# Attention over a compressed memory, then a SwiGLU layer: the column of ones that sums the exponentials is made 32 columns wide

## The chip, the core and the metric

The kernel runs on one core of one Trainium2 chip. Its engines work side by side, each through its own queue in order: TensorE (PE; its weight loads are listed apart, as PEld), VectorE (DVE), ScalarE (ACT), GpSimd (POOL), and SyncE (SP), which issues the DMAs. On-chip data lie in SBUF; TensorE writes its results to PSUM. The metric is the time of one execution on the device, in microseconds, as the median of several runs. A profile is one further execution, recorded by the hardware profiler.

## The reference

Eight batches of eight heads with 576 tokens of 64 values. For each of 32 memory slots, a softmax of `phi` over the tokens weighs k and v into a summary row, 32 rows a head; q attends to those rows; the result, 4608 tokens of 512 values, goes through an RMS norm and a SwiGLU layer of width 1536. All is float32.

```python
def _attn_ref(q, k, v, phi):
    a = phi - np.max(phi, axis=2, keepdims=True)
    a = np.exp(a)
    a = a / (np.sum(a, axis=2, keepdims=True) + 1e-09)
    k_m = np.einsum('bhsm,bhsd->bhmd', a, k)
    v_m = np.einsum('bhsm,bhsd->bhmd', a, v)
    ...
    return np.matmul(attn, v_m)

def _moe_ref(x, w_gate, w_val, w_out, rms_g):
    ...
    g = xn @ w_gate
    silu = g * (1.0 / (1.0 + np.exp(-g)))
    val = xn @ w_val
    return (silu * val @ w_out)
```

(What is left out first is the scores of q against `k_m` and their softmax over the slots, `attn`; then the RMS norm.) `phi` is laid out with axis 2 as the 576 tokens, so the sum in the third line of `_attn_ref` runs over the tokens: one number for each head and slot.

## The kernel before

**Stages.** The batches are numbered 0 to 7 and worked on in pairs. For each batch the kernel loads `phi`, k and v (`load_phi`, `load_kv`), takes the maximum of `phi`, subtracts it and exponentiates (`prep`), and multiplies the exponentials with k and v (`kv_steps`). Queries are scored against the result (`q_steps`, `score_steps`), normed (`x_steps`), and multiplied with the weights of the SwiGLU layer (`vw_steps`, `gv_steps`, `out_steps`). The weights come in as `raw` and are split by integer arithmetic on DVE into two halves of lower precision (`convert`, with lines 413 to 443 on DVE). In the first 165 us these stages overlap; from there on nearly all is the SwiGLU layer, with some attention of the last two pairs in between.

**Order.** The order of the instructions is written out by hand. Each step has a number, its place; all steps are sorted by place and issued in that order. `K_AT` has the places of the eight batches' products, `KP` the distance of two of their six chunks, and `POST` the places of what follows them: `sums`, `post1`, `turn`, `post2`, `self_products`, `post3`. SP issues the loads in an order of its own, each behind the one before.

**The sums.** `e_bd` holds a batch's exponentials, for four pairs of heads and nine groups of 128 rows (64 tokens of each of the two heads), as 128 x 64 blocks whose columns are the 32 slots of each head. `chunk` (line 787) multiplies each block with the 128 columns of k and v of the same rows and adds them up in the PSUM tile `kvp`, columns 0 to 127; even and odd pairs (`par`) go to the upper and the lower 64 rows of the tile, which are two column halves of TensorE's array. `prep` (line 764) has POOL add some of the nine blocks together into `es`; `ESN` says how many such additions there are for a batch. `sums` (line 802) then multiplies what is left, 7, 5 or 3 blocks for each pair of heads, with a tile `ones` of 128 x 1, and adds them up in column 128 of `kvp`. All products of one pair of heads follow each other before the next pair's, in the other half, begin. Over all batches that is 36 blocks for each of four pairs, 144 products.

**What reads them.** `post1` (lines 810 to 814) adds 1e-9 to column 128 and writes that to column 129 (`si`), takes the reciprocal (`ri`), and scales columns 0 to 127 with it (`kn`). `turn` (line 824) transposes `kn`, and `post2` copies it to `km` and `vt`, for the scores and for the SwiGLU layer.

Of the kernel before, what the change touches and what calls it, by code (L numbers as in the profile page):

```python
# [8 lines left out]
F32 = mybir.dt.float32  # L9
# [10 lines left out]
WB = 4  # L20
PRM = dict(
    LK=150,
    V0=169.536,
    V0S=[-7.546, 0.266, 0.444],
    G0=[3.08, 8.562, 9.611, 9.895],
# [83 lines left out]
def kernel(  # L109
# [26 lines left out]
    P = 128  # L136
# [13 lines left out]
    persist = ctx.enter_context(tc.tile_pool(name="persist", bufs=1))  # L150
# [380 lines left out]
    def vw_steps(i, vp_tile=None):  # L531

        ps_, u, pr, j = where(i)

        def mm(cc):
            def f():
                if cc == 0:
                    vp_[i] = vp_tile() if vp_tile else ps.tile([P, 2, 2, 256], F32, tag="vw", name=f"vp{i}", bufs=1)
                vp = vp_[i]
                vh, vl = vm[pr][:, 0], vm[pr][:, 1]  # L540
                wh, wl = (x.rearrange("p hp g f -> p hp (g f)") for x in wsplit[ps_ * NJ + j])
                for e in range(2):
                    def lhs(vt):
                        return vt[:, cc, e].rearrange("p o x -> p (o x)")
                    for n, (l, r) in enumerate(((vh, wh), (vh, wl), (vl, wh))):
                        nc.tensor.matmul(  # L546
                            vp[:, cc, e, :], lhs(l), r[:, 2 * cc + e, :],
                            start=(n == 0), stop=(n == 2),
                        )
            return f  # L550

        def evac():
            vp = vp_.pop(i)
            xh, xl = (x.rearrange("p e c f -> p c e f") for x in slot(i))
            for h in range(2):
                rows = slice(64 * h, 64 * h + 64)
                src = vp[rows, :, ::-1, :] if h else vp[rows]
                nc.scalar.copy(xh[rows], src)  # L558
                urgent.append(nc.vector.tensor_tensor(  # L559
                    out=xl[rows], in0=src, in1=xh[rows].bitcast(F32), op=ALU.subtract  # L560
                ).ins)
        return [mm(0), mm(1), evac]
# [61 lines left out]
    with ExitStack() as c1:  # L624
# [5 lines left out]
        c1k = ExitStack()  # L630
        sk = c1k.enter_context(tc.tile_pool(name="sbk", bufs=2, side="right", reuse_waits="tile"))

        ones = persist.tile([P, 1], F32, name="ones")
        nc.vector.memset(ones, 1.0)
        a_tiles = {0: sa.tile([P, NT, 256], F32, name="a0", bufs=1)}

# [38 lines left out]
        def load_kv(b, hp):  # L675
            if b in HOME:
                if ("kvx", b, hp // 2) not in st:
                    st["kvx", b, hp // 2] = persist.tile(
                        [P, 2, 2, S], F32, tag=f"at{'hl'[hp // 2]}{HOME[b]}", name=f"kv{b}_{hp // 2}x"
                    )  # L680
                t = st["kvx", b, hp // 2][:, hp % 2]
            else:
                t = sk.tile([P, 2, S], F32, tag="kv", name=f"kv{b}_{hp}", bufs=PRM["KB"])
            for i, src in enumerate((k, v)):
                load(
                    t[:, i, :],
                    src[b, 2 * hp:2 * hp + 2].rearrange("h (p c) d -> (h p) (c d)", c=NT),
                )
            st["kv", b, hp] = t
# [86 lines left out]
        def kv_steps(b):  # L776
# [18 lines left out]
            def sums():  # L795
                kvp = st["kvp", b]
                for cc in range(2):
                    for par in range(2):
                        hp = 2 * cc + (par ^ j)
                        es = st["es", b]  # L800
                        for i, x in enumerate(es):
                            nc.tensor.matmul(
                                kvp[64 * par:64 * par + 64, cc, 128:129],
                                x[:, hp, :], ones, start=(i == 0), stop=(i == len(es) - 1),
                            )

            def post1():
                kvp = st["kvp", b]
                si = kvp[:, :, 129:130]
                nc.vector.tensor_scalar_add(si, kvp[:, :, 128:129], 1e-9)  # L810
                ri = sb.tile([P, 2, 1], F32, tag="ri", name=f"ri{b}")
                nc.vector.reciprocal(ri, si)
                st["kn", b] = kn = sb.tile([P, 2, P], F32, tag="kn", name=f"kn{b}")
                nc.vector.tensor_tensor(
                    out=kn, in0=kvp[:, :, 0:P], in1=ri.broadcast_to([P, 2, P]), op=ALU.mult
                )
# [58 lines left out]
            for cc in range(2):  # L875
                for c0 in range(0, NT, 3):
                    steps.append(chunk(cc, c0, c0 + 3))
            return steps, [sums, post1, turn, post2, self_products, post3], store

        def q_steps(pr, s):  # L880
# [94 lines left out]
        def place(base, offsets, steps):  # L975
            assert len(offsets) == len(steps)
            return [(base + o, f) for o, f in zip(offsets, steps)]
# [8 lines left out]
        for b in range(B):  # L986
            steps, post, store = kv_steps(b)
            if b >= 2 * G:
                ev.append((max(K_AT[b] + 6 * PRM["KP"] + PRM["POST"][5] + PRM["VD"][b - 2 * G], PRM["LK"]), store))
            ev += place(K_AT[b], [PRM["KP"] * i for i in range(6)], steps)  # L990
            ev += place(K_AT[b] + 6 * PRM["KP"], PRM["POST"], post)
            for hp in range(HP):
                if (b, hp) > (0, 1):
                    ev.append((min(K_AT[b] + PRM["KD"][b * HP + hp], PRM["LK"] - 0.1), lambda b=b, hp=hp: load_kv(b, hp)))
            if b == 0:
# [26 lines left out]
        def s_tile(name, shape):  # L1022
            return ps_s.tile(shape, F32, tag="S", name=name, bufs=PRM["B"][2])
        ev += place(PRM["V0"], PRM["V0S"], vw_steps(0, lambda: s_tile("vp0", [P, 2, 2, 256])))
        gv0 = gv_steps(0, lambda name: s_tile(name, [P, 1024]))
        ev += place(PRM["V0"], PRM["G0"], [gv0[x] for x in (0, 1, 3, 4)])
        if PRM["E1"]:
            ev += place(PRM["V0"], PRM["V1"], vw_steps(1, lambda: s_tile("vp1", [P, 2, 2, 256])))
        close = K_AT[B - 1] + 6 * PRM["KP"] + 0.1
# [298 lines left out]
```

## Time and profile before

| what | value |
|---|---|
| timed runs (3) | 857.08, 855.59, 855.20 us; median 855.59 us |
| the profiled execution | 850.64 us |
| its span, first to last instruction | 848.9 us |
| granted TensorE clock, mean over the span | 0.989 |
| busy: PE, weight loads, DVE, ACT, POOL | 812.3, 731.9, 537.0, 403.7, 322.9 us |
| DMA | 131.62 MB, mean 155 GB/s |

The page of the profile has, after the busy times, one line for each engine with its busy share in 40 equal slices, and the clock that TensorE was granted in them. Its fourth part follows the chain that ended last back from the last instruction: at each step to what released it, or to the instruction before it on its engine. A group of instructions is told by line, engine, operation and tiles (`out<-in`, the program's names without their numbers), with partitions x columns of the array for TensorE, the size of what it streams, and the count; behind the bar stand busy time, the mean duration of one in ns, and the idle time of the engine just before. Matmuls are pipelined and overlap, so durations of neighbours don't add up, and where one half of the array works beside the other two of them run at once. A few per cent of the matmul records can be missing.

### The profile page before, as it was taken

How to read it: one execution, taken by the hardware profiler on the slowest of the kernel's cores; microseconds unless marked ns; L12 is line 12 of the kernel's file. 1: busy time of each engine (PE TensorE's matmuls, PEld its weight loads, DVE VectorE, ACT ScalarE, POOL GpSimd, SP SyncE). 2: the span in 40 equal slices, each digit the busy share in tenths (PEclk: the TensorE clock that was granted, in tenths of full speed). 3: DMA queues.
4: the chain of work that ended last, by engine and by line, in shares of the span. 5: the costliest groups of instructions: out<-in, count | busy, mean ns of one | idle time of the engine just before them, and what ended most of it. 6: DMA issues, size and time to landing. Idle time of an engine off the chain costs nothing.

```text
span 848.9 us, 16232 instructions
## 1 busy us (share of the span) xinstructions
PE 812.3 (96%) x6234; PEld 731.9 (86%) x6234; DVE 537.0 (63%) x940; ACT 403.7 (48%) x731; POOL 322.9 (38%) x279
## 2 busy tenths in 40 slices
PE   5989997999999999999999989999999999999997
PEld 4878886889989889988989888899999999999996
DVE  5697868876678898979889546312354454444434
ACT  2767647687565465656454423354333223232220
POOL 3565746734444563643544512411212122121220
PEclk9889999999999999999999999999999999999999
DMA  9997525545343543743534567806736357264437
GB/s 335 364 383 271 201 72 152 149 117 153 115 119 96 167 124 78 189 132 104 150 111 130 176 144 198 239 15 168 180 94 179 77 149 199 59 153 88 100 100 174
DMA packets 99493, 131.62 MB, mean 155 GB/s; under 512 B 42324, under 2 KB 61784, under 8 KB 99416
## 3 DMA queue, kind: packets, MB, share of 16 engines
q1 hardware_dynamic: 99416, 130.59, 54.6%
q8 instruction: 49, 0.80, 0.4%
q14 instruction: 28, 0.23, 0.1%
HBM read 73.93 MB, written 31.46 MB: 124 GB/s over the span
## 4 chain that ended last, share of the span: by engine, by line
PE 74%; DVE 9%; DMA 5%; ACT 3%; issue 3%; POOL 3%; SPq 2%; ACTq 0%; POOLq 0%; DVEq 0%
PE po L1120 31%; PE pg L586 14%; PE pv L586 14%; PE vp L546 3%; PE vq L1059 3%; PE kvp L787 2%; SPq L1102 1%; DVE xl L559 1%; DMA kv_0x<-in_k_dram 1%; DVE mi L438 1%; DVE ex L413 1%; DVE ex L416 1%; PE S L1199 1%; PE xp L280 1%; ACT xh L558 1%
## 5 line engine op out<-in xcount | busy, mean ns | idle before, releaser
L614 POOL TENSOR_TENSOR hl<-hf,hh 128x512 fp32r<-128x512 f32 (+1 forms) x86 | 124.5, 1449 | 285.7 <-ACT hh L613 285.6
L1128 DVE TENSOR_TENSOR acc<-po,acc 128x512 f32<-128x512 f32 x180 | 123.5, 688 | 124.2 <-PE po L1120 123.5
L1120 PE MATMUL po<-oh,hh 128*128 128x512 f32 x387 | 154.1, 399 | 4.5 <-DVE at L246 1.9
L1120 PE MATMUL po<-ol,hh 128*128 128x512 f32 x387 | 153.3, 396 | 0.5 <-DMA ol<-od 0.5
L1120 PE MATMUL po<-oh,hl 128*128 128x512 f32 x387 | 151.5, 391 | 0.0
L595 DVE TENSOR_TENSOR hf<-pv,sg 128x320 f32<-128x320 f32 (+1 forms) x188 | 83.4, 452 | 88.4 <-PE pv L586 64.3
L594 ACT ACTIVATE sg<-pg 128x320 f32<-128x320 f32 (+1 forms) x188 | 76.6, 410 | 123.4 <-PE pg L586 115.2
L586 PE MATMUL pg<-ath,xh 128*128 128x320 f32 (+1 forms) x376 | 85.9, 301 | 3.9 <-ACT sg L594 3.6
L1120 PEld LDWEIGHTS po<-oh,hh 128*128 128x128 f32 x387 | 73.0, 189 | 16.9 <-DVE at L246 2.1
L1120 PEld LDWEIGHTS po<-oh,hl 128*128 128x128 f32 x387 | 73.0, 189 | 16.1
L586 PE MATMUL pg<-ath,xl 128*128 128x256 f32 (+1 forms) x376 | 83.8, 297 | 0.7 <-DMA xl<-sl 0.7
L613 ACT CAST hh<-hf 128x512 fp32r<-128x512 f32 (+1 forms) x86 | 57.4, 672 | 55.2 <-DVE hf L595 37.6
L586 PE MATMUL pv<-ath,xl 128*128 128x256 f32 (+1 forms) x376 | 82.9, 296 | 0.0
L586 PE MATMUL pg<-atl,xh 128*128 128x256 f32 (+1 forms) x376 | 82.9, 297 | 0.0
L586 PE MATMUL pv<-ath,xh 128*128 128x320 f32 (+1 forms) x376 | 82.2, 298 | 0.4 <-DVE hf L595 0.3
L586 PE MATMUL pv<-atl,xh 128*128 128x256 f32 (+1 forms) x376 | 81.6, 296 | 0.0
L1120 PEld LDWEIGHTS po<-ol,hh 128*128 128x128 f32 x387 | 73.1, 189 | 9.0 <-DMA ol<-od 0.7
L462 POOL TENSOR_TENSOR w<-mi,ex 128x512 f32<-128x512 f32 x34 | 43.9, 1290 | 84.8 <-ACT mi L450 54.6
L586 PEld LDWEIGHTS pg<-ath,xh 128*128 128x128 f32 x376 | 62.6, 189 | 9.2 <-ACT sg L594 4.3
L559 DVE TENSOR_TENSOR xl<-vp,xh 64x1024 fp32r<-64x1024 f32 x48 | 58.5, 1219 | 16.4 <-ACT xh L558 15.6
L586 PEld LDWEIGHTS pv<-ath,xh 128*128 128x128 f32 x376 | 61.6, 189 | 3.6 <-DVE hf L595 0.9
L586 PEld LDWEIGHTS pg<-ath,xl 128*128 128x128 f32 x376 | 62.2, 190 | 2.8 <-DMA xl<-sl 0.9
(163 smaller groups left out, 1519.7 us busy)
## 6 DMA issues: line engine op xcount, KB each, us to landing
xh<-sh SPq DMA_DIRECT2D x96, 128.0 KB, 3.7
xl<-sl SPq DMA_DIRECT2D x80, 128.0 KB, 3.1
out_dram<-acc SPq DMA_DIRECT2D x72, 128.0 KB, 2.4
raw<-in_moe_w_gate_dram SPq DMA_DIRECT2D x12, 512.0 KB, 4.0
raw<-in_moe_w_val_dram SPq DMA_DIRECT2D x12, 512.0 KB, 3.8
raw<-in_moe_w_out_dram SPq DMA_DIRECT2D x12, 512.0 KB, 4.0
wd<-whl SPq DMA_DIRECT2D x24, 256.0 KB, 3.8
whl<-wd SPq DMA_DIRECT2D x12, 512.0 KB, 5.3
```

What stands on the lines that cost most here:

```text
L462: (nc.gpsimd if on_pool else V).tensor_tensor(out=d["w"], in0=m, in1=ex, op=ALU.mult)
L546: nc.tensor.matmul(vp[:, cc, e, :], lhs(l), r[:, 2 * cc + e, :], start=(n == 0), stop=(n == 2),)
L559: urgent.append(nc.vector.tensor_tensor(out=xl[rows], in0=src, in1=xh[rows].bitcast(F32), op=ALU.subtract).ins)
L586: nc.tensor.matmul(pt[:, :N], l[cc][:, b, half * P:half * P + P], r[:, cc, b, t0:t0 + n, :].rearrange("p t x -> p (t x)"), start=(m == 0), ...
L594: nc.scalar.activation(sg[:, :N], pg[:, :N], AF.Silu)
L595: urgent.append(nc.vector.tensor_tensor(out=hf[:, :, b, :], in0=pv[:, :N].rearrange("p (t x) -> p t x", x=64), in1=sg[:, :N].rearrange("p ...
L613: nc.scalar.copy(hh, hv)
L614: nc.gpsimd.tensor_tensor(out=hl, in0=hv, in1=hh.bitcast(F32), op=ALU.subtract)
L787: nc.tensor.matmul(kvp[64 * par:64 * par + 64, cc, 0:128], e_bd[j][:, hp, c, :], st["kv", b, hp][:, :, 64 * c:64 * c + 64], start=(c == 0) ...
L1059: nc.tensor.matmul(vp[:, h, e, :], vall[a][:, cc, k:k + 4, :].rearrange("p q m -> p (q m)"), w, start=(a == 0), stop=(a == 1),)
L1120: nc.tensor.matmul(po, l[:, tt, :], r, start=(m == 0), stop=(m == 5))
L1128: nc.vector.tensor_tensor(out=accs[key], in0=po, in1=accs[key], op=ALU.add).ins
```

## The change

The tile `ones` becomes 128 x 32, all 1.0, and so each product in `sums` writes 32 equal columns, 128 to 159, in place of column 128 alone. `post1` still reads column 128; its own column `si` moves from 129 to 160. The tile `kvp` has 256 columns for each two pairs of heads, so it doesn't grow.

```diff
 PRM = dict(
     LK=150,
+    W1=32,
...
-        ones = persist.tile([P, 1], F32, name="ones")
+        ones = persist.tile([P, PRM["W1"]], F32, name="ones")
         nc.vector.memset(ones, 1.0)
...
                             nc.tensor.matmul(
-                                kvp[64 * par:64 * par + 64, cc, 128:129],
+                                kvp[64 * par:64 * par + 64, cc, 128:128 + PRM["W1"]],
                                 x[:, hp, :], ones, start=(i == 0), stop=(i == len(es) - 1),
                             )
 
             def post1():
                 kvp = st["kvp", b]
-                si = kvp[:, :, 129:130]
+                si = kvp[:, :, 128 + PRM["W1"]:129 + PRM["W1"]]
                 nc.vector.tensor_scalar_add(si, kvp[:, :, 128:129], 1e-9)
```

## The prediction

> **What bounds the kernel now.** I read the page first: the span and the chain of waits by engine.
>
> ```profile
> span 848.9 us, 16232 instructions
> ...
> PE 74%; DVE 9%; DMA 5%; ACT 3%; issue 3%; POOL 3%; SPq 2%; ACTq 0%; POOLq 0%; DVEq 0%
> ```
>
> The chain is TensorE for three quarters of the span, so anything that slows TensorE or its clock there counts. Next come the instructions that read the ones (the view by tile; min/median/max in ns, then first and last start), and the sums' pieces of the chain in order of time (start, length).
>
> ```profile
> L802 PE MATMUL kvp<-ones,e_bd x160: 197/197/246, 18.1 to 124.1; 128*64 128x1 f32 x160
> L802 PE MATMUL kvp<-ones,es x128: 167/197/218, 17.8 to 124.0; 128*64 128x1 f32 x128
> ```
>
> ```profile
> 69.56 1.80 PE kvp L802 x38
> ...
> 72.39 0.73 PE kvp L802 x11
> ...
> 73.29 0.59 PE S L918 x18
> ...
> 94.90 0.68 PE kvp L802 x19
> ...
> 105.14 0.68 PE kvp L802 x19
> ```
>
> There are 160 + 128 = 288 matmuls of one column, two instructions for each fp32 product, each with its own weight load of 64 columns, and all in the first 125 us. On the later chain lie 38 + 11 + 19 + 19 = 87 of them, in 3.89 us, between other pieces of TensorE. (S is there for a comparison below.)
>
> Then I read the clock by stretches, cut where it changes; the columns are start:end, length, busy time of PE, weight loads, DVE, ACT and POOL, clock, DMA share and GB/s.
>
> ```profile
> 16.97:20.39 3.42, 3.42 (x72) 3.23 (x69) 2.62 (x3) 1.17 (x2) 0.00 (x0) 1.00 1.08 395
> 20.39:27.21 6.82, 5.73 (x53) 5.38 (x54) 3.83 (x11) 4.63 (x4) 3.81 (x3) 0.50 0.96 329
> 27.21:47.69 20.48, 17.95 (x320) 15.72 (x317) 15.74 (x25) 17.03 (x33) 11.08 (x12) 1.00 1.06 379
> 47.69:54.52 6.83, 6.28 (x59) 5.10 (x59) 6.71 (x12) 4.09 (x12) 5.07 (x6) 0.50 1.07 383
> 146.68:150.09 3.41, 3.41 (x12) 2.83 (x12) 3.09 (x6) 3.41 (x8) 2.99 (x2) 0.50 0.00 0
> ```
>
> Half clock is granted three times, for 6.82, 6.83 and 3.41 us, so the clock seems to be judged in windows of 3.41 us. Ahead of the first drop stands a window in which PE counts as busy for all of its 3.42 us.
>
> **What the change adds: wider matmuls.** Each of the 288 streams 31 columns more. What a column costs is bounded by two neighbouring rows, with the same 64-column weights and 64 or 128 columns streamed.
>
> ```profile
> L918 PE MATMUL S<-km,qT x288: 219/223/368, 32.8 to 97.6; 128*64 128x64 f32 x144
> L787 PE MATMUL kvp<-kv,e_bd x216: 272/273/323, 34.5 to 123.3; 128*64 128x128 f32 x108
> ```
>
> By the first a column is (223 - 197) / 63 = 0.41 ns, by the second (273 - 197) / 127 = 0.60 ns: 13 to 19 ns of duration for 31 columns. What the path pays is the spacing, not the duration. The weight loads of the first group of sums show that:
>
> ```profile
> 18.03 0.49 PEld L802 LDWEIGHTS kvp<-ones,e_bd 128*64 128x64 f32 x7
> ```
>
> Seven loads in 0.49 us overlap heavily. With some 0.14 us for the last, they start (0.49 - 0.14) / 6 = 58 ns apart, all in one column half of the array. S switches halves at every product and does 18 in 0.59 us, 33 ns each, so at most 66 ns apart in one half, with 64 columns. From 1 to 64 columns the spacing in a half thus grows by at most 8 ns, and 31 columns are half of that: at most 4 ns, 87 x 4 = 0.35 us. A streaming time of 13 ns fits into the 58 ns that go by between two loads anyway. I take 1 ns: **+0.1 us**. The upper end is that nothing hides: 87 x 13 = 1.1 us to 87 x 19 = 1.7 us. The lower end is that wide sums issue as densely as S does, 3.89 us - 87 x 33 ns = 1.0 us less. I don't take it, since S gets its 33 ns from switching halves at every step, which the sums still won't do.
>
> The rest is small. The memset writes 32 columns instead of one, once, while the first loads are on their way: nothing, and some tens of ns if that cover were gone. The last matmul of a group ends 13 to 19 ns later ahead of DVE, in the three or four groups on the chain: **+0.05 us**. The `si` column moves within its tile, and DVE's operations on it keep their shapes. No wait, DMA or buffer is added, and no queue changes its order.
>
> **What the change moves: the clock.** The columns streamed in a window tell more than the busy time does. These are the matmuls from 16.97 to 20.39 us, after which the clock fell; then those of the window from 68.17 to 71.58 us, after which it held (groups by form: count, busy us, mean ns, idle before).
>
> ```profile
> L802 PE MATMUL kvp<-ones,e_bd 128*64 128x1 f32 x39 | 2.5, 198 | 0.0
> L802 PE MATMUL kvp<-ones,es 128*64 128x1 f32 x16 | 1.6, 202 | 0.0
> L787 PE MATMUL kvp<-kv_1x,e_bd 128*64 128x128 f32 x12 | 1.1, 277 | 0.0
> L733 PE MATMUL mr<-ident,mx 128*64 128x128 f32 x4 | 0.4, 272 | 0.0
> ```
>
> ```profile
> L802 PE MATMUL kvp<-ones,e_bd 128*64 128x1 f32 x30 | 1.9, 197 | 0.0
> L802 PE MATMUL kvp<-ones,es 128*64 128x1 f32 x12 | 1.1, 198 | 0.0
> L787 PE MATMUL kvp<-kv_1x,e_bd 128*64 128x128 f32 x10 | 0.9, 283 | 0.0
> L897 PE MATMUL qtp<-ident,qr 128*128 128x128 f32 x5 | 0.8, 284 | 0.0
> L218 PE MATMUL tp<-ident,a 128*128 128x128 f32 x3 | 0.5, 291 | 0.0
> ```
>
> The first streams 55 + 16 x 128 = 2,103 columns, the second 42 + 18 x 128 = 2,346. With 32 columns the first has 55 x 32 + 2,048 = 3,808. So I expect **no drop at 20.39 us**. Against this reading stands the third drop. Its window, from 143.27 us on, has at least 8 x 256 columns of these two kinds, and up to 512 of a third that starts at its end, so up to 2,560, and still lost the clock, with 1.9 us of plain idling in it: columns alone aren't the whole rule.
>
> ```profile
> L586 PE MATMUL pg<-ath,xh 128*128 128x256 f32 x4 | 0.9, 311 | 0.0
> L546 PE MATMUL vp<-whl,vm 128*128 128x256 f32 x4 | 0.6, 282 | 0.0
> L1120 PE MATMUL po<-oh,hh 128*128 128x512 f32 x1 | 0.6, 598 | 1.9 <-DVE at L246 1.9
> ```
>
> In the Trainium skill's "TensorE: Matmul & The Clock Gate", the section "What's actually happening" has the gate follow how busy the PE has been. If that meant matmuls in flight, the full window at 16.97 could not have lost the clock, and the change would leave the clock alone; by the rows, one-column matmuls count for little. Either way the sum below comes out the same to 0.1 us.
>
> For the price of that drop is nearly nothing. The products of the second batch run in it:
>
> ```profile
> L787 PE MATMUL kvp<-kv_0x,e_bd 128*64 128x128 f32 x36 | 4.1, 421 | 0.0
> ```
>
> At full clock that would be about half, so what follows on PE could come some 2 us sooner. But who is late next? DVE, whose pieces are here, with SP's issue of a load and, from the view of the DMA issues, its size and its us to landing:
>
> ```profile
> 34.58 1.36 DVE L742 TENSOR_TENSOR phi<-phi,mr 128x1152 f32<-128x1152 f32 x1 [1.34 <-PE mr L733]
> 35.85 0.47 DVE L413 TENSOR_SCALAR ex<-raw 128x512 int32<-128x512 int32 x1
> ```
>
> ```profile
> 28.93 0.38 SPq L348 DMA_DIRECT2D raw<-in_moe_w_gate_dram  x1
> ```
>
> ```profile
> raw<-in_moe_w_gate_dram SPq DMA_DIRECT2D x1, 512.0 KB, 6.8
> ```
>
> ```profile
> DVE ex L430 <- ACT ex L419: 0.2, 1, 0.2
> ```
>
> DVE's wait for PE, 1.34 us up to 34.58, would go. But the raw weights land at 28.93 + 6.8 = 35.7 us, and L413 reads them at 35.85. The queues already move 379 GB/s at a share of 1.06 there, so the load can't land sooner. From L413 on DVE waits for others only once up to 63 us, 0.2 us for ACT (the last fence, of the waits from 34.6 to 63 us). So the gain is **-0.1 us** at L413; if DVE found other inputs, up to 2 us. The drop at 47.69 comes while DVE is the late one and stays.
>
> **The sum** against the profiled execution's 850.64 us (848.9 of span, 1.7 around it): + 0.1 + 0.05 - 0.1, no change. The median of the timed runs, 855.59 us, lies 4.95 us above that execution; carried over, the forecast is **855.5 us**.
>
> **The rivals.** *Faster: a drop that this profile just missed.* A window laid from 69.6 to 73.0 us, 1.4 us later than the one above, holds this:
>
> ```profile
> L802 PE MATMUL kvp<-ones,e_bd 128*64 128x1 f32 x38 | 2.5, 197 | 0.0
> L802 PE MATMUL kvp<-ones,es 128*64 128x1 f32 x12 | 1.2, 202 | 0.0
> L218 PE MATMUL tp<-ident,a 128*128 128x128 f32 x4 | 0.7, 286 | 0.0
> L897 PE MATMUL qtp<-ident,qr 128*128 128x128 f32 x4 | 0.6, 272 | 0.0
> ```
>
> That is 50 + 8 x 128 = 1,074 columns, half of what lost the clock at 20.39; with 32 columns 2,624. If the windows lie otherwise in other executions, the old kernel loses half of 3.41 us (1.7 us), or of two windows (3.4 us), in a stretch where the chain is TensorE, and the new one doesn't. For it: the timed runs spread over 1.9 us and lie above the profiled one. Against it: one profile can't show that the windows move, and DVE and ACT may take up part. In the same section the Trainium skill calls the window free-running; nothing in this trace can show that. Time: 855.6 - 1.7 = 853.9 to 855.6 - 3.4 = 852.2 us. Chance 0.30.
>
> *Slower: the columns aren't hidden.* If the next weight load in a half waits until the last column has streamed, the 87 sums on the chain pay 13 to 19 ns each: 856.7 to 857.3 us. It passes 0.2% (1.7 us, about what a measurement of this kernel can tell from no change) at 20 ns each. For it: the sums run several times in a row in one half. Against it: S, at 66 ns with 64 columns. Chance 0.10, with whatever else turns out worse in the order of waits.
>
> *It does nothing to the clock.* The drop at 20.39 stays, because PE idles soon after the sums anyway (5.73 us busy of 6.82). The time is 855.6 and falls into the forecast: a third of its chance.
>
> **How the numbers follow.** Same 0.60 (853.9 to 857.3), faster 0.30, slower 0.10. The range reaches down over the faster rival, two windows lost before and none after, to 852.0, and up to the middle of the slower one, 857.0.
>
> **What would show it.** The sums' loads still 58 ns apart in a half, and 38 of them in about 1.8 us, show the columns hidden; 71 ns or more shows the slower rival. Full clock from 20.39 to 27.21 us with L413 still near 35.8 us shows the cap. I would be wrong if DVE's work after 36 us moved forward with PE, or if the clock of the two kernels differs near 72 us from one execution to the next.

## The result

The changed kernel takes 862.22 us (median of 9 runs, 857.37 to 865.33), the kernel before 855.59 us in the same comparison: a ratio of 1.007 with an interval of 1.0048 to 1.0093. It is slower, by about 6.6 us, and outside the forecast range. Its profiled execution took 859.45 us. The page of the profile of the changed kernel, span and chain by engine:

```profile
span 857.7 us, 16234 instructions
...
PE 78%; DVE 8%; ACT 4%; POOL 3%; DMA 3%; issue 2%; SPq 2%; POOLq 0%; DVEq 0%; ACTq 0%
```

The work is the same but for the wider products; lines behind 23 have moved down by one. The view by tile shows the products themselves (min/median/max in ns):

```profile
L803 PEld LDWEIGHTS kvp<-ones,e_bd x160: 132/138/227, 19.3 to 130.2; 128*64 128x64 f32 x160
L803 PE MATMUL kvp<-ones,e_bd x160: 192/223/294, 19.4 to 130.2; 128*64 128x32 f32 x160
L635 DVE MEMSET ones<- x1: 85/85/85, 0.8 to 0.8; 128x32 f32 x1
```

A product lasts 223 ns where it lasted 197, but that is duration, not spacing. The chain of waits of the changed kernel, in order of time (start, length), has this piece:

```profile
111.32 0.68 PE kvp L803 x19
```

Nineteen sums in 0.68 us, as before (105.14 and 94.90 there). The columns are hidden; that isn't where 6 us went.

**Where they went.** The last sums of batch 3 end at 60.96 us before and at 59.77 after: the changed kernel is ahead. Those of batch 5 end at 95.57 and 101.74, and from there to batch 7 both need 28.7 us. So about 7.4 us are lost between 60 and 102 us (41.97 us from batch 3 to batch 5 in place of 34.61). Behind batch 7 the changed kernel needs 727.3 us, the kernel before 724.6 in this profile and 727.3 in a second one (experiment e8), so that part needn't be the change's. The waits of TensorE from 60 to 102 us in the changed kernel (us in total, times, longest):

```profile
PE qtp L898 <- ACT qT L906: 1.8, 1, 1.8
PE mr L734 <- DVE mx L725: 1.6, 1, 1.6
PE xp L281 <- ACT at L229: 1.1, 1, 1.1
PE mt L717 <- DVE mc L710: 0.6, 1, 0.6
PE qtp L898 <- DVE at L229: 0.3, 1, 0.3
```

and those from 60 to 98 us in that second profile of the kernel before:

```profile
PE qtp L897 <- DVE at L228: 0.7, 1, 0.7
PE xp L280 <- ACT at L228: 0.7, 1, 0.7
PE kvt L824 <- DVE kn L814: 0.4, 1, 0.4
```

5.4 us of waiting in place of 1.8, for other producers. The two programs hold the same operations on every engine. What changed is the order in which they stand. The launch at the end of the file (line 1324) builds the program so:

```python
    with _tile.TileContext(nc, schedule_with_timeline_sim=True) as tc:
```

The places that the kernel section above calls the order are only the order in which the program hands its instructions over. A scheduler then orders them, by modelled times as its name says; that a product of 32 columns has another modelled time than one of a single column is what e3 and e4 below bear out. The two built programs differ in their order on every engine. On PE the differences run from the 97th to the 642nd of 5,288 matmuls (an fp32 product, which the trace shows as two instructions, counts once), on DVE from the 19th to the 128th of 940 operations: from the first batch's sums to batch 5's products. On PE ahead of batch 4's products (lines of the changed kernel; before at the left, after at the right):

```
L717 mt  (maxima, batch 5)               L717 mt
L825 kvt x8                              L734 mr x2
L788 kvp, products of batch 4 x15        L898 qtp_0_4 x4
L734 mr x2                               L825 kvt x8
L898 qtp_0_4 x4                          L788 kvp, products of batch 4 x9
```

Ahead of the first score `S` of the next pair there stand more transposes and `xp` products than before (8 `xp`, 5 `qtp` and 4 `tp` more). And at batch 5 the transpose `qtp_3_8` stands ahead of all products; before, it stood behind the first 17.

### The profile page after: what moved, and what is told of

It is laid out like the page before. It is cut to its first block, busy times and chain, and to the rows that moved or that the text cites. A ratio compares the mean times of both kernels' runs of the same rounds, so it can differ in the third digit from the quotient of the medians.

```text
span 857.7 us, 16234 instructions
## 1 busy us (share of the span) xinstructions
PE 819.1 (96%) x6234; PEld 734.0 (86%) x6234; DVE 537.2 (63%) x940; ACT 403.9 (47%) x731; POOL 322.2 (38%) x279
## 4 chain that ended last, share of the span: by engine, by line
PE 78%; DVE 8%; ACT 4%; POOL 3%; DMA 3%; issue 2%; SPq 2%; POOLq 0%; DVEq 0%; ACTq 0%
PE po L1121 32%; PE pg L587 15%; PE pv L587 15%; PE vp L547 4%; PE vq L1060 3%; PE kvp L788 3%; SPq L1103 1%; PE S L1200 1%; DVE mc L710 1%; PE kvp L803 1%; DVE xl L560 1%; DMA phi<-in_phi_dram 1%; PE gv L587 1%; PE tp L219 1%; PE xp L281 1%
## 5 line engine op out<-in xcount | busy, mean ns | idle before, releaser
L614 ACT CAST hh<-hf 128x512 fp32r<-128x512 f32 (+1 forms) x86 | 57.4, 672 | 55.0 <-DVE hf L596 37.5
```

The lines of the kernel that those rows point to most:

```text
L614: nc.scalar.copy(hh, hv)
```

## The experiments

Where the width of the sums had to be set apart from the order, the sums were widened or narrowed after the order was settled:

```python
def _set_width(nc, n):
    ...
    i = copy.replace(i, ins=[wide(i.ins[0]), *i.ins[1:]], outs=[wide(i.outs[0])])
```

so that all instructions stand as they would with the other width. "Old order" is that of the kernel before, "new order" that of the changed one.

### e1: 32 columns in the old order

```diff
-                                kvp[64 * par:64 * par + 64, cc, 128:128 + PRM["W1"]],
-                                x[:, hp, :], ones, start=(i == 0), stop=(i == len(es) - 1),
+                                kvp[64 * par:64 * par + 64, cc, 128:129],
+                                x[:, hp, :], ones[:, 0:1], start=(i == 0), stop=(i == len(es) - 1),
...
+    _set_width(nc, 32)
```

> All 144 sums are 32 columns wide, but every engine's instructions stand in the order of the kernel before: the sums are widened after the order is settled. Theory A (the changed order of the instructions costs the time, not the columns): the time of before, ratio 0.996 to 1.002, some 855 us beside 855.6, and sums at 38 in about 1.8 us. Theory B (the 31 more columns cost it, on TensorE): the time of the changed kernel, ratio 1.007, some 862 us. If the clock stays up at 20.4 us here, that part of the prediction holds by itself.

Measured: 857.48 us, ratio 1.0017 (0.9999 to 1.0035). The longest piece of sums on its chain is as long as before:

```profile
71.97 1.80 PE kvp L803 x38
```

All 87 sums on the chain take 3.92 us (1.80 + 0.76 + 0.68 + 0.68), in the kernel before 3.89. And the half clock of 20.39 us is gone: it is granted at 15.84, ahead of batch 0's sums, and then not before 43.14.

### e2: one column in the new order

```diff
+    _set_width(nc, 1)
```

(added to the changed kernel)

> The order of the changed kernel, but each sum is one column wide, narrowed after the order is settled. Theory A: as slow as the changed kernel, ratio 1.007 (1.004 to 1.010), some 862 us. Theory B: the time of before, ratio 1.000.

Measured: 866.28 us, ratio 1.0110 (1.0081 to 1.0139). All sums are as narrow as before, and it is the slowest kernel of all, slower than either theory expected. With e1 that settles the first question: the loss is the order's, not the columns'.

### e3 and e4: which batch's sums turn the order

```diff
-                                x[:, hp, :], ones, start=(i == 0), stop=(i == len(es) - 1),
+                                x[:, hp, :], ones[:, :(PRM["W1"] if b == 0 else 1)], start=(i == 0), stop=(i == len(es) - 1),
```

(the output slice likewise; e4 has `b >= 1`)

> Only the 28 sums of batch 0 are 32 columns wide; the other 116 have one column. Every engine's order is that of the changed kernel. Theory A: ratio 1.007 (1.004 to 1.010), some 862 us. Theory B: 28 of 144 sums, and none of them on the later chain, so no more than a fifth of the cost, ratio 1.000 to 1.0015.

> The 116 sums of batches 1 to 7 are 32 columns wide, those of batch 0 have one column. Every engine's order is that of before. Theory A: ratio 0.997 to 1.002. Theory B: at least the share of the sums that lie on the later chain, ratio 1.005 to 1.007.

Measured: e3, with batch 0 alone wide, has the new order, 861.30 us, ratio 1.0067 (1.0041 to 1.0093). e4, with the seven other batches wide, has the old order, 857.07 us, ratio 1.0014 (0.9993 to 1.0034). In the built programs four columns in batch 0 are enough to turn the order, and two are not.

### e5, e6, e7: the new order in pieces

Other widths at the time when the order is settled turn only parts of it. All three kernels then run with 32 columns everywhere:

```diff
-    W1=32,
+    W1=120, W=[32, 1, 1, 104, 1, 1, 1, 1],
...
+    _set_width(nc, 32)
```

(the slices in `sums` take `PRM["W"][b]`) for e5 (the new order up to batch 3, the old one at the two places shown above); `W=[32, 1, 1, 40, 1, 1, 1, 1]` for e6 (the place at batch 4 new as well, but with 4 `xp` products and one transpose fewer ahead of the first `S` than in the whole new order) and `W=[1, 1, 1, 96, 1, 1, 1, 1]` for e7 (of the two places only the one at batch 5 new, and the early part old).

> All 144 sums have 32 columns. The order is the new one up to batch 3, and the old one at the two spots that look costly: the row maxima's transposes (mr) of batch 5 stand behind the first 14 products of batch 4 again, not ahead of them, and the last transposes of the queries (qtp_3_8) stand within batch 5's products, not ahead. Theory A (the order costs at these two spots, and its early part gains about 1 us, as the first four groups of sums ended 1.2 us sooner): 854 to 857 us, ratio 0.998 to 1.002, and PE's idle gaps of 1.6 us near 63 us and 1.8 us near 93 us are gone. Theory B (the new order costs throughout, or in its early part): 860 to 863 us, ratio 1.005 to 1.009.

> As the run with the early part alone, but the spot at batch 4 has the new order too (mr ahead of all products of batch 4); the spot at batch 5 stays old. Theory A: PE waits about 2 us for DVE's maxima near 62 us again (L725), and with the half clock that followed there it costs 2 to 4 us against the early part alone: 857 to 860 us, ratio 1.002 to 1.005. If nearly all of the loss is at batch 5, it is the same as the early part alone, 854 to 857 us; if nearly all is at batch 4, 860 to 863 us.

> All sums have 32 columns. The order is the old one up to batch 4's products; at batch 5 the transposes qtp_3_8 stand ahead of all products, as in the new order. Theory A: PE waits for ACT's qT (L906) near 93 us about 1 to 2 us longer than before, and with the half clock behind it that costs 2 to 4 us: 858 to 861 us, ratio 1.003 to 1.006. If the spot at batch 5 is harmless by itself (PE was only late there because it had come late from batch 4): as the old order with wide sums, 855 to 858 us, ratio 0.999 to 1.003.

Measured: e5 851.74 us, ratio 0.9961 (0.9941 to 0.9980); e6 854.09 us, 0.9977 (0.9959 to 0.9994); e7 856.49 us, 1.0008 (0.9991 to 1.0026). The early part of the new order costs nothing; the kernel with it alone is faster than both, and faster than either theory expected. Each of the two places by itself costs little: e6 against e5 2.4 us, with intervals that overlap, and e7 against e1 nothing, though the wait for ACT that was expected there is in its profile (1.5 us). The whole new order loses 0.9% against e6 and 1.1% against e5 (1.0070 against 0.9977 and 0.9961). Another expectation of e5 failed: waits of 2.1 and 1.4 us near 62 us are still there, so such waits, which looked like a good part of the loss, are not. A limit of the method: the nudge moves more than the place it is named for (on PE, e6 and the changed kernel differ at many places from the 412th to the 642nd matmul, from batch 4's products on). And no run has the early part with the place at batch 5 alone.

### e8: the kernel before again

> The kernel before, once more, for a profile on the same chip as these runs. If the windows in which the clock is judged lie the same in every execution, the clock falls at 20.39, 47.69 and 146.68 us again. If they run free, the drops lie elsewhere, by up to 3.4 us, and one more may come or go. By both, the sums of batch 7 end near 124 us, and no gap of PE over 1 us lies between 60 and 96 us.

Measured: 855.17 us in its single run; span 853.4 us. Half clock was granted at 15.43, 22.26, 49.57, 128.07, 141.73, 169.03 and 506.95 us, in place of 20.39, 47.69 and 146.68. So the windows of 3.41 us lie differently in these two executions. Batch 7's sums end at 126.09 us, 2 us later than expected; batch 0's began 1.8 us later too (19.57 against 17.8 us).

### e9 to e12: the early order again, and the changed kernel beside it

e9 is e5 with `_set_width(nc, 1)`. e10 is e5 without it, so that its widths stay 32, 1, 1, 104, 1, 1, 1, 1. e11 has 88 in place of 104, which moves one product of batch 4 behind `mr` and `qtp`. e12 is the changed kernel.

> Exactly the order of the run with the early part alone, instruction for instruction on all five engines, but every sum has one column. If the width itself is worth something through the clock behind batch 0's sums (in the new order the narrow run was some 4 us slower than the wide one, with the clock halved at 17.55 and at 24.38 us), it is slower than the wide run of this order by 2 to 4 us, 854 to 856 us, ratio 0.998 to 1.000. If the width is worth nothing by itself: the same as that run, 850 to 853.5 us, ratio 0.994 to 0.998.

> The order of the run with the early part alone again, now with the widths that give that order left as they are: 32 columns for batch 0, 104 for batch 3, one for the others. It tells whether that order is really faster, with batch 0 wide. If it is: 850 to 854 us, ratio 0.994 to 0.998. If the first of these runs was lucky in where the half-speed windows fell: 855 to 857 us, ratio 0.999 to 1.002.

> All sums have 32 columns; the order of the run with the early part alone, but for one product of batch 4 that stands behind the transposes mr and qtp in place of ahead of them. By the theory that the order at this spot costs only when the transposes stand ahead of all products: the same as that run, 850 to 854 us, ratio 0.994 to 0.998.

> The changed kernel once more, on the same chip as the last runs of the early order, for a like-with-like profile. Time: ratio 1.005 to 1.009 to the kernel before. In its profile the sums of batch 3 end 36 to 38 us behind those of batch 0 and those of batch 5 then 41 to 43 us later, where the kernel before has 40 and 34.6; if the half-speed windows lie elsewhere, the half clock in batch 5's products (5.60 us for 72) may be gone, and then the second stretch is 40 to 41.5 us.

Measured: e9 856.85 us, ratio 1.0010 (0.9990 to 1.0031), a little above what was expected; e10 854.08 us, 0.9978 (0.9957 to 1.0000); e11 853.14 us, 0.9973 (0.9947 to 0.9998); e12 861.91 us, 1.0070 (1.0044 to 1.0096). The early order is faster than the kernel before in three kernels (e5, e10, e11), by 0.2 to 0.4%, as long as batch 0's sums are wide; e10's interval reaches 1.0000. Narrow, it isn't. The second stretch of e12, 44.5 us in the table below, is longer than the 41 to 43 us expected.

The runs side by side, with the time from the end of batch 0's sums to batch 3's and from there to batch 5's in each profile (the ends of the last `kvp<-ones` products):

| order | width | kernel | ratio | 0 to 3, us | 3 to 5, us |
|---|---|---|---|---|---|
| old | 1 | before (first profile; e8) | 1 | 40.3; 40.4 | 34.6; 34.6 |
| old | 32 | e1 | 1.0017 | 40.7 | 34.7 |
| old | 1 at batch 0, 32 | e4 | 1.0014 | 38.6 | 36.1 |
| old, batch 5 new | 32 | e7 | 1.0008 | 39.2 | 36.8 |
| early part new | 32 | e5 | 0.9961 | 36.4 | 38.6 |
| early part new | 32 | e11 | 0.9973 | 36.9 | 39.8 |
| early part new | 32, 104 or 1 | e10 | 0.9978 | 38.5 | 34.7 |
| early part new | 1 | e9 | 1.0010 | 40.5 | 37.6 |
| early part and batch 4 new | 32 | e6 | 0.9977 | 37.5 | 38.2 |
| new | 32 | after; e12 | 1.0070 | 37.4; 37.0 | 42.0; 44.5 |
| new | 32 at batch 0, 1 | e3 | 1.0067 | 36.4 | 43.0 |
| new | 1 | e2 | 1.0110 | 37.6 | 44.6 |

Added up, the two stretches take 74.9 us in the kernel before, 73.2 to 76.7 in the kernels with another order and batch 0 wide (e5, e6, e7, e10, e11), and 79.3 to 82.2 with the whole new order. The early part brings up to 4 us by batch 3 and gives it back by batch 5, in e11 more than all of it; in e10, where it brings 1.8 us, it keeps 1.7. The second stretch of the whole new order is 7 to 10 us longer than before.

**How the two places may work together.** What follows is read from the profiles; no run tests it apart. e11 and e12 ran on the same chip and stand level at 57.5 and 57.7 us, where batch 3's sums end. Here is TensorE in e11 (start, busy, count, and the idle time before with its releaser):

```profile
75.13 0.28 PE L919 MATMUL S<-km,qT 128*64 128x64 f32 x1
...
88.42 1.09 PE L281 MATMUL xp<-gb,at 128*64 128x128 f32 x16 [0.68 <-ACT at L229]
...
90.89 0.66 PE L898 MATMUL qtp<-ident,qr 128*128 128x128 f32 x4 [0.56 <-DVE at L229]
...
91.96 2.13 PE L788 MATMUL kvp<-kv,e_bd 128*64 128x128 f32 x34
```

and in e12:

```profile
78.86 0.57 PE L919 MATMUL S<-km,qT 128*64 128x64 f32 x10
...
90.17 1.09 PE L281 MATMUL xp<-gb,at 128*64 128x128 f32 x16 [1.15 <-ACT at L229]
...
93.92 0.66 PE L898 MATMUL qtp<-ident,qr 128*128 128x128 f32 x4 [1.84 <-ACT qT L906]
94.88 0.33 PE L898 MATMUL qtp<-ident,qr 128*128 128x128 f32 x1 [0.31 <-DVE at L229]
95.14 0.66 PE L281 MATMUL xp<-gb,at 128*64 128x128 f32 x8
95.63 1.79 PE L788 MATMUL kvp<-kv,e_bd 128*64 128x128 f32 x16
```

(the last row is cut off by the end of the view).

First, at batch 4, the scores `S` start 3.7 us later, behind all that now stands ahead of them. DVE, which needs them, has little to do. Windows of e12 (start:end, length, busy time of PE, weight loads, DVE, ACT and POOL, clock):

```profile
72.00:76.00 4.00, 4.00 (x59) 3.32 (x58) 1.17 (x3) 2.23 (x6) 0.79 (x2) 1.00 0.90 296
76.00:80.00 4.00, 4.00 (x61) 3.39 (x61) 1.31 (x6) 2.21 (x4) 2.19 (x2) 1.00 0.94 313
...
88.00:92.00 4.00, 2.85 (x40) 2.21 (x38) 3.98 (x9) 2.80 (x4) 2.60 (x4) 1.00 0.02 4
92.00:96.00 4.00, 1.85 (x20) 1.42 (x21) 3.93 (x9) 2.85 (x6) 2.12 (x5) 0.97 0.00 0
```

and of e11:

```profile
72.00:76.00 4.00, 4.00 (x80) 3.79 (x80) 2.86 (x5) 3.16 (x5) 0.91 (x1) 1.00 1.05 385
76.00:80.00 4.00, 4.00 (x66) 3.30 (x63) 2.22 (x7) 2.21 (x4) 2.91 (x3) 1.00 0.71 245
...
88.00:92.00 4.00, 3.02 (x36) 2.45 (x38) 4.00 (x9) 3.23 (x4) 1.34 (x5) 1.00 0.00 0
92.00:96.00 4.00, 4.00 (x71) 3.71 (x67) 3.86 (x11) 2.38 (x8) 2.61 (x3) 1.00 0.20 50
```

From 72 to 80 us DVE is busy 2.5 of 8 us in e12 and 5.1 in e11, while TensorE is full in both: DVE falls behind there without one idle moment of TensorE. Between 88 and 96 us DVE is full in both, and TensorE is busy 4.7 of 8 us in e12, 7.0 in e11. But an empty DVE alone isn't the loss: in e6, at the same distance from batch 0's sums (74.7 to 82.7 us), DVE is busy only 3.1 of 8 us, and e6 loses little.

Second, at batch 5, transposes wait for copies that stand behind long work on ACT and DVE. ACT in e12:

```profile
90.34 2.34 ACT L753 ACTIVATE e_bd<-phi 64x1152 f32<-64x1152 f32 x2 [0.23 <-DVE phi L743]
92.71 0.68 ACT L939 ACTIVATE ex<-ex 128x576 f32<-128x576 f32 x1
93.30 0.57 ACT L906 COPY qT<-qtp 128x512 f32<-128x512 f32 x1
```

The `qtp` at 91.47 is copied out only at 93.30, behind 3 us of exponentials, and the next `qtp` waits for that copy: the 1.84 us above. ACT has the same order in e6, but there the next `qtp` starts ahead of the copy:

```profile
92.72 0.66 PE L898 MATMUL qtp<-ident,qr 128*128 128x128 f32 x4 [0.50 <-DVE at L229]
```

```profile
93.88 1.05 ACT L906 COPY qT<-qtp 128x512 f32<-128x512 f32 x2
```

In the source, `qtp`, `tp`, `mt` and `mr` take turns in two PSUM buffers (`tag="tr"`), so the order of the transposes also settles whose copy frees the buffer for the next one: DVE's `at` in e6, ACT's `qT` in e12. The chain of e12 goes through DVE:

```profile
92.49 2.01 DVE mc L710
94.50 0.34 DVE at L229
...
94.88 0.33 PE qtp L898
95.21 0.59 PE xp L281 x8
95.80 5.60 PE kvp L788 x72
```

A reduction of 2.01 us, `mc`, a maximum for a later batch, stands ahead of the 0.34-us copy `at`. `qtp_3_8` and the 8 `xp` instructions behind it wait for that copy, and batch 5's 72 products stand behind them. The place of `qtp_3_8` itself adds 0.33 us to the chain. The chain of e6, with the old order at this place:

```profile
92.38 0.29 DVE at L229
...
92.72 0.66 PE qtp L898 x4
93.37 0.59 PE xp L281 x8
93.96 1.96 PE kvp L788 x34
95.92 0.26 PE qtp L898
```

There, too, the `xp` products stand ahead of batch 5's, but the copy comes ahead of the reduction, so `mc` isn't on the chain at all. (Its scores are hardly late, though: counted from the end of batch 0's sums they start at 55.0 us, in e11 at 54.5, in e12 at 58.1.) On the chain of e12 the time from 83.4 to 94.8 us is nearly all ACT's and DVE's; of e6 it is TensorE's for most of it.

This second place alone isn't the loss either. In e7 `mc` stands ahead of `at` and on the chain as in e12 (1.98 us, from 89.81), and TensorE waits 1.5 us for ACT's copy and 1.0 us for DVE's; its second stretch is 2.1 us longer than e1's, and its time is e1's. What only the whole new order has in these profiles is DVE late from batch 4 and then the reduction ahead of the copy; that the two add up to the loss is argued, not shown.

By starts of the same work, e12 falls behind e11 by 0.65 us up to the maxima's transposes `mr` (86.72 and 87.37), 1.75 at `xp` (88.42, 90.17), 3.03 at the next `qtp` (90.89, 93.92), 3.67 at the products. The products then meet a half-speed window from 95.76 us on (5.60 us for 72; e11 takes 4.36 from 92.13 to 96.49 with a `qtp` in between), and at the end of batch 5's sums the difference is 97.35 to 102.20, 4.85 us. In the 3.41 us ahead of that window TensorE was busy for 1.53. The loss doesn't need the half clock: e3 has none there, does its 72 products in 3.93 us, and still needs 43.0 us from batch 3 to batch 5.

## Why the prediction was wrong, by its steps

**The step that failed: "no queue changes its order."** I read the places in the source as the order of the program. They are only what the scheduler is handed. The change reorders all five engines' instructions. e1 has the change without the new order, 1.0017 (0.9999 to 1.0035); the new order with one column has 1.0110. The slower rival had the right sign by the wrong mechanism: it priced uncovered columns, and "whatever else turns out worse in the order of waits" was left without a price.

**Wider matmuls, +0.1 us: right as far as the runs can tell.** The 87 sums on the chain take 3.92 us in e1 and 3.89 before; weight loads stay at 138 ns. From batch 3 to batch 5 e1 needs 34.7 us, the kernel before 34.6. The memset, 85 ns at 0.8 us, is out of the way. e1 and e4 leave room for up to 0.35% that I can't place.

**The clock behind batch 0's sums: right.** In the five profiles with batch 0 narrow (before, e2, e4, e8, e9) a half-speed window begins behind the start of these sums and before 40 us, or (e4) the clock stays halved until 32.01 us. In the nine with batch 0 wide (after, e1, e3, e5, e6, e7, e10, e11, e12) none does; the next one comes at 43.14 us or later. The windows of e9 and of e11 behind these sums (e9 narrow, e11 wide):

```profile
22.39:29.22 6.83, 5.74 (x54) 5.48 (x56) 4.47 (x11) 4.34 (x4) 3.81 (x3) 0.50 0.73 250
```

```profile
20.63:61.21 40.58, 32.74 (x588) 29.21 (x588) 32.51 (x57) 29.96 (x54) 24.09 (x28) 1.00 1.05 371
```

**Its price, -0.1 us by the cap at L413: right in the old order, and the exception that I named came true in the new one.** DVE in e1:

```profile
33.97 1.36 DVE L743 TENSOR_TENSOR phi<-phi,mr 128x1152 f32<-128x1152 f32 x1 [1.34 <-PE mr L734]
38.06 0.43 DVE L414 TENSOR_SCALAR ex<-raw 128x512 int32<-128x512 int32 x1 [2.73 <-DMA raw<-in_moe_w_gate_dram]
```

DVE's wait of 1.34 us for PE, which the prediction saw going, is still there, but DVE comes to it 11.4 us behind the end of batch 0's sums in place of 13.9. It is early and then waits 2.73 us for the raw weights: the gain ends at that landing. In the early order (e11) the scores' work fills that hole:

```profile
34.76 0.76 DVE L930 TENSOR_REDUCE mxs<-S 128x18 f32<-128x576 f32 x1 [0.32 <-PE S L919]
35.55 0.76 DVE L932 TENSOR_TENSOR ex<-S,mxs 128x576 f32<-128x576 f32 x1
36.23 0.42 DVE L414 TENSOR_SCALAR ex<-raw 128x512 int32<-128x512 int32 x1
```

"If DVE found other inputs, up to 2 us" was the condition. Counted from the end of batch 0's sums, the first raw weights are read after 15.2 and 15.3 us in the old order narrow (before, e8) and 15.5 wide (e1), but after 17.9 us in the early order narrow (e9) and 15.6 wide (e11). There the width is worth 0.3 to 0.5% (e10, e11 and e5 against e9, 2.8 to 5.1 us), more than the 2 us; the intervals of e10 and e11 overlap with e9's a little. In the whole new order it is 0.4% (e3 and e12 against e2).

**The faster rival.** That the windows lie otherwise in other executions is shown (the kernel before has its first full-speed stretch from 13.56 us in one profile and from 12.02 in the other). That agrees with the Trainium skill, "TensorE: Matmul & The Clock Gate", section "What's actually happening", which calls the window free-running. But the narrow sums near 72 us lost the clock in neither profile of the kernel before, and e1, without narrow sums, isn't faster.

**What stays open.** The profiles show e12 4.9 us behind e11 at batch 5 and 5.9 us at the end, the timed medians 8.8 us; where the rest goes isn't seen in one execution each. Nor do single profiles show where the early order's 0.2 to 0.4% come from: at batch 7's sums e5 and e11 stand level with e8 (125.84, 126.06 and 126.09 us).

## What to carry to other kernels

Where a program is ordered by modelled times, a change of a size or shape can also be a change of order: compare the order of both built programs before arguing about the edited instructions, and measure the edit in the old order. In such a kernel an order can be worth more than the edit (here 1.1% between two orders of the same instructions), so try some orders by harmless nudges; e5, e10 and e11 came out 0.2 to 0.4% ahead of the kernel before that way. And a busy TensorE doesn't mean that nothing is being lost: look at what its work feeds.

## What the runs showed of the hardware

A TensorE that the profile counts as fully busy can be kept at half clock. In e4, with batch 0's sums alone narrow, the clock stayed halved for five windows in a row, from 14.94 to 32.01 us, among them these:

```profile
18.35:21.77 3.42, 3.42 (x37) 3.07 (x33) 1.30 (x2) 0.00 (x0) 0.00 (x0) 0.50 1.06 394
21.77:25.18 3.41, 3.41 (x45) 3.41 (x46) 2.40 (x7) 2.32 (x2) 0.59 (x1) 0.50 0.41 147
```

Both are full of matmuls: of the first window's 37, 14 have one column, of the second's 45 all have. In none of the nine profiles with 32 columns in the same place did the clock stay halved behind these sums or fall there.
